# The second product of the last pair of token blocks as seven block products

## The chip, the cores and the metric

The kernel runs on one core of one Trainium2 chip. The metric is the device time of one execution in microseconds (us); three runs of the kernel before gave 1180.23, 1180.44 and 1181.78 us, median 1180.44. The engines are called as the profile calls them: PE is TensorE's matmul side and PEld its weight loads, DVE is VectorE, ACT is ScalarE, POOL is GpSimd, and SP issues the transfers.

## What is computed

Attention with a short window and block summaries runs first; its output is a matrix `x` of 3072 tokens by 512. A mixture of four experts follows, and it holds nearly all the matmul work:

```python
def _moe_ref(x, domain_probs, w1, w2):
    p = domain_probs / (domain_probs.sum(-1, keepdims=True) + 1e-09)
    for e in range(E):                      # E = 4
        h = np.maximum(x @ w1[e], 0.0)      # 512 -> 1024, the first product
        out += p[:, e:e+1] * (h @ w2[e])    # 1024 -> 512, the second product
```

## The kernel before, in words

The tokens are cut into 8 blocks of 384 (`TB`). Blocks 0 and 1 are done with plain products in 32-bit operands. The other six make three pairs (`PAIRS`, line 893), each pair going through the four experts in the order that is listed there; pair 3 takes experts 3, 2, 1, 0. In the pairs every operand is scaled and split in two 16-bit floats, a high part and the rest, and a product of two matrices is three matmul passes: high by high, high by rest, rest by high.

**First product of a pair** (`first`, line 1025). For one expert it goes over four blocks of 256 hidden columns (`order`, four values of `i`). Each block is a 2x2 block product done in seven block products instead of eight (Strassen's scheme in Winograd's form, `SEVEN`, line 989): seven groups of six matmuls with 384 columns. The sums of blocks that it needs are made ahead: those of `x` in `x_operands` (line 453) and those of `w1` in `w1_operands` (line 816). Four PSUM banks a, b, c, d hold the running sums. After product 0, ACT copies bank a to b; after product 1 it copies d to a tile in SBUF; DVE makes c from b after product 2 and d from b after product 4. So product 2 waits for the copy that follows product 0, and product 4 for DVE's reading of b after product 2. Each finished quarter goes through `to_h` (line 855): ACT writes the high part with the Relu, DVE the rest.

**Second product** (`mm2`, line 867). For each of the six tiles of 128 tokens in a pair, 8 hidden groups by 3 passes make 24 matmuls of 512 columns into one bank; DVE then adds the bank, times the mixing weight, to the tile's sum `acc` (line 888), and after the last expert SP stores it (line 890). In `pair_units` (line 994) the second product of one expert is interleaved with the first product of the next; that of the last expert stands alone. The high and low parts of `w2` were made for pair 1, stored to DRAM, and are read back for pairs 2 and 3 (`w2_scaled`, line 776; `fetch2`, line 919), one transfer for two hidden groups. The expert that ends one pair begins the next, and its `w2` stays in place.

**What sets the order.** The program is written as generators that yield after each piece of matmul work, and attention's steps are placed between by their due times; all of attention is done by the end of pair 2. What is written is then ordered by a scheduler at build time: it gives every engine a list in which an instruction may stand well before its written place, as soon as its inputs and a free buffer are there; pieces inside `tc.high_priority` (line 1059) go first. On the chip each engine runs its list in order, so an instruction that waits holds up all that stands behind it. Buffers are counted by tag: 8 of tag `w2`, 14 of tag `x` (`NX`), 7 of tag `w1`, 4 raw weight tiles `wr`, and 16 each of `hh` and `hl`.

Of the kernel before, what the change touches and what calls it, by code (L numbers as in the profile page):

```python
# [26 lines left out]
TB = 384  # L27
NTB = B * S // TB
KC = DM // P
FC = DF // P  # L30
# [13 lines left out]
NX = 14  # L44
# [18 lines left out]
def attn_moe(ctx: ExitStack, tc: tile.TileContext, qvL, qv0, v0L, kD, kT, vT, w1L, w2L, dpL, cst, out):  # L63
# [18 lines left out]
    V, A, PL, PE = (Engine(e, "rest") for e in (nc.vector, nc.scalar, nc.gpsimd, nc.tensor))  # L82
    SP = Engine(nc.sync, "load")

    def pool(name, bufs=1, **kw):
        return ctx.enter_context(tc.tile_pool(name=name, bufs=bufs, **kw))
# [7 lines left out]
    sb = pool("sb")  # L94
    ps_mm = pool("ps_mm", 4, space=bass.MemoryType.PSUM)
    ps_sc = pool("ps_sc", 2, space=bass.MemoryType.PSUM)
    ps_av = pool("ps_av", 2, space=bass.MemoryType.PSUM)
# [9 lines left out]

    X_TOP, W1_TOP = 8.0, 0.25  # L110
    V_TOP = 256.0
    ones = const.tile([2, P], F32, name="ones")
    V.memset(ones, 1.0)
# [1 line left out]
    scale_w, back_w, scale_v, back_x = {}, {}, {}, {}  # L115
# [307 lines left out]
    def x_half(name, dtype=F32R):  # L423
        return sb.tile([P, 2, TB], dtype, name=name, tag="x", bufs=NX)
# [26 lines left out]
    XS = ("11", "21", "22", "t1", "t2", "t3", "t4")  # L451

    def x_operands(pr):
        xp = {w: [x_half(f"x{v}{pr}_{w}", F16) for v in "hl"] for w in XS}

        def split(w, raw, c, lo):
            hi, low = (x[:, :, c : c + QB] for x in xp[w])
            A.copy(hi, raw)
            lo.tensor_tensor(low, raw, hi, op=ALU.subtract)

        def part(ib):
            raw = sb.tile([P, 4, 2, QB], F32, name=f"xr{pr}_{ib}", tag="chunk", bufs=CHUNKS)
            SP.dma_start(raw, xraw.pop((pr, ib)))
            b11, b12, b21, b22 = (raw[:, k] for k in range(4))
            c = ib * QB
            split("11", b11, c, PL)
            V.tensor_tensor(b11, b12, b11, op=ALU.subtract)
            split("22", b22, c, PL)
            V.tensor_tensor(b12, b22, b12, op=ALU.subtract)
            V.tensor_tensor(b22, b22, b11, op=ALU.subtract)  # L470
            split("t2", b22, c, V)
            split("t1", b11, c, PL)
            split("t3", b12, c, V)
            split("21", b21, c, PL)
# [260 lines left out]
    RUSH = 200  # L735
    SLOW = 0.6
    US1, US2 = 0.175, 0.231

    def load_weights(src, e, fc, which):
        raw = sb.tile([P, 512], F32, name=f"wr{which}{e}_{fc}", tag="wr", bufs=4)  # L740
        SP.dma_start(raw, src[e, fc])
        return raw
# [73 lines left out]
    def w1_operands(e, pr):  # L816
# [30 lines left out]
            later(8, SP.dma_start, stored[e, pr, "1"][j], group)  # L847
        return ws

    acc, added = {}, {}  # L850
    scaled_pw = {}
    xpair = {}
    kept = {}
# [37 lines left out]
        yield done, 1.0  # L891

    PAIRS = ((1, (3, 2, 1, 0)), (2, (0, 1, 2, 3)), (3, (3, 2, 1, 0)))

    es_of = dict(PAIRS)
    orders, todo, ready = {}, [], {}
    before = None
    for pr, es in PAIRS:  # L900
        for e in es:
# [11 lines left out]
                return  # L913


    todo2 = [(pr, e, j) for pr, es in PAIRS for e in es for j in range(FC // 2) if pr == 1 or e != es[0]]
    ready2 = {}

    def fetch2():
        if todo2:  # L920
            pr, e, j = todo2.pop(0)
            ready2.setdefault((pr, e), {}).update(w2_scaled(e, j))
# [9 lines left out]
    def tile_by_tile(tbs, e, hT, w2):  # L932
        for tb in tbs:
            for t in range(TB // P):
                yield from mm2(tb, e, [t], hT, w2, range(FC))
# [9 lines left out]
    def plain_units(tbs, e, early=0, last=False):  # L945
# [43 lines left out]
    SEVEN = (  # L989
        ("a", "11", "11"), ("d", "s1", "t1"), ("b", "s2", "t2"), ("a", "12", "21"),  # L990
        ("b", "s3", "t3"), ("c", "s4", "22"), ("b", "22", "t4"),
    )

    def pair_units(pr, es, last=False):


        tbs = (2 * pr, 2 * pr + 1)
        behind = None
        for n, e in enumerate(es):
            hT = {}  # L1000
            w2 = kept.pop(e)[1] if pr > 1 and e in kept else ready2.setdefault((pr, e), {})
            kept.clear()
            units = first(pr, tbs, e, hT, w2, "hl"[n % 2])
            if behind is None:
                for us in units:
                    yield us, SLOW
            else:
                todo_us = 0.0
                for us in units:
                    yield us, 1.0  # L1010
                    todo_us += us * second_share
                    while todo_us > 0.0:
                        us2, _ = next(behind, (todo_us, 0))
                        todo_us -= us2
                        if _:
                            yield us2, 1.0
                yield from behind
            if n < len(es) - 1:
                behind = tile_by_tile(tbs, e, hT, w2)
        kept[e] = {}, w2  # L1020
        yield from with_fetch(second(tbs, e, hT, w2, last))

    second_share = 2 * (TB // P) * FC * 3 * US2 / (2 * FC * 3 * KC * US1 * 7 / 8)

    def first(pr, tbs, e, hT, w2, room):
        xp = xpair[pr]
        room_h = "h" + room
        scaled_pw[e] = sb.tile([P, S // P, 1], F32, name=f"pw{pr}_{e}", tag="pws", bufs=3)
        V.tensor_scalar(
            scaled_pw[e], pw[:, pr * (S // P) : (pr + 1) * (S // P), e : e + 1], back_w[e], back_x[pr],  # L1030
            op0=ALU.mult, op1=ALU.mult,
        )
        order = orders[pr, e]
        for n, i in enumerate(order):
            fetch((pr, e, i))
            if n < len(order) - 1:
                fetch((pr, e, order[n + 1]))
            elif e != es_of[pr][-1]:
                fetch()
            f1, f2 = 2 * i, 2 * i + 1  # L1040
            bank = {}

            def new(k):
                room, tag = dict(a=(ps_sc, "sc"), d=(ps_av, "av")).get(k, (ps_mm, "mm"))
                bank[k] = room.tile([P, 512], F32, name=f"ph{k}{pr}_{e}_{i}", tag=tag)[:, :TB]
                return bank[k]

            for m, (k, w, x) in enumerate(SEVEN):
                first = m < 2
                o = new(k) if first else bank[k]  # L1050
                wh, wl = (ready[pr, e, i][w][:, v * 256 : (v + 1) * 256].rearrange("p (c f) -> p c f", f=P) for v in range(2))
                xh, xl = xp[x]
                again = dict(skip_group_check=not first)
                for c in range(2):
                    PE.matmul(o, wh[:, c, :], xh[:, c, :], start=c == 0 and first, stop=False, **again)
                    PE.matmul(o, wh[:, c, :], xl[:, c, :], start=False, stop=False, **again)
                    PE.matmul(o, wl[:, c, :], xh[:, c, :], start=False, stop=c == 1, **again)
                ahead_of = ExitStack()
                ahead_of.enter_context(tc.high_priority(offset=RUSH))
                if m == 0:  # L1060
                    A.copy(new("b"), o)
                elif m == 1:
                    five = sb.tile([P, TB], F32, name=f"p5{pr}_{e}_{i}", tag="hs", bufs=2)
                    A.copy(five, o)
                elif m == 2:
                    V.tensor_tensor(new("c"), o, five, op=ALU.add)
                elif m == 3:
                    to_h(hT, tbs[0], e, f1, o, room_h)
                elif m == 4:
                    V.tensor_tensor(bank["d"], o, five, op=ALU.add)  # L1070
                    to_h(hT, tbs[1], e, f2, bank["d"], room_h)
                elif m == 5:
                    to_h(hT, tbs[1], e, f1, o, room_h)
                else:
                    to_h(hT, tbs[0], e, f2, o, room_h)
                ahead_of.close()
                if m == 3:
                    if len(w2) < FC:
                        fetch2()
                yield 6 * US1  # L1080
# [3 lines left out]
    for n in range(per, NTB * per):  # L1084
        k = n + SHIFT * (n >= 2 * per)
# [11 lines left out]
    for b in range(1, B):  # L1097
        k = 2 * per * b + SHIFT
        steps += [(k - 2.0, setup_k, b), (k - (0.65 if b == 1 else 1.3), setup_v, b)]
    steps.sort(key=lambda s: s[0])  # L1100
    at = 0
# [18 lines left out]

    plan = [([0], (0, 1)), ([1], (1, 0)), ([0, 1], (2, 3)), *PAIRS]
    pos = per
    for (tbs, experts), end in zip(plan, ENDS):
        pair = tbs if isinstance(tbs, int) else None
        n = 2 if pair else len(tbs)
# [5 lines left out]
        parts, u, done = None, 0.0, 0.0  # L1131
# [82 lines left out]
```

## Time and profile before

| | |
|---|---|
| median of three runs | 1180.44 us |
| the profiled execution, first to last instruction | 1179.2 us |
| pair 3, first matmul to last matmul | 941.6 to 1175.2 us |
| the lone second product at the end of pair 2 | 910.9 to 941.5 us |
| pairs 1 and 2, roughly | 380 to 620 and 620 to 910 us |

The profiled execution's own span, 1179.2 us, is 1.2 us below the median. The page gives busy time for each engine over the span and in 40 slices of 29.5 us; a digit is the busy share in tenths. A row of a group reads: line, engine, operation, what is written from what, shape, count, then busy time, the mean duration of one, and the idle time before. Nearly all rows say L75, since a helper on that line issues every operation, so the tile names tell them apart: `po` are the banks of the second product, `pha` to `phd` those of the first product in pairs, `h` the split hidden values, `wr` raw weights, `w1g` and `w2s` prepared weights, `p` the tile that holds the copy of d.

### The profile page before, as it was taken

To read this page: it belongs to the slowest core of one execution; us is meant where nothing else is said; L and a number is where in the kernel's file an instruction comes from. 1 tells how busy PE (TensorE), PEld (TensorE's weight loads), DVE (VectorE), ACT (ScalarE), POOL (GpSimd) and SP (SyncE) were. 2 spreads that over 40 slices of the span, in tenths; PEclk is the share of its full clock that TensorE was granted. 3 is DMA by queue.
4 is the path that set the end of the run, shared out by engine and by line. 5 is a ranking of instruction groups with operands and counts; after the bars stand their busy time and mean duration, and the time that the engine had idled before them with its cause. 6 is when DMAs were issued, how large, how long until landed. Compare 5 with 4: busy or idle time off the path is not lost.

```text
span 1179.2 us, 19097 instructions
## 1 busy us (share of the span) xinstructions
PE 1114.9 (95%) x6562; PEld 715.7 (61%) x6562; DVE 709.1 (60%) x1767; ACT 598.4 (51%) x1682; POOL 455.3 (39%) x554
## 2 busy tenths in 40 slices
PE   9899698999999888989979999999999999999998
PEld 7788587798897544444545455555555455555553
DVE  6877879875889767666886754554455343322221
ACT  5767466664557687777664454444443132111110
POOL 2588466762736777675642321222111100000000
PEclk9999889999999899999989999999999999999999
DMA  6576656653845767786773554463633132324001
GB/s 240 157 207 181 172 155 185 171 155 92 250 110 150 227 214 261 245 251 209 229 250 110 176 149 135 126 191 111 201 103 96 64 118 72 118 86 122 28 1 54
DMA packets 166417, 181.90 MB, mean 154 GB/s; under 512 B 79024, under 2 KB 114864, under 8 KB 166320
## 3 DMA queue, kind: packets, MB, share of 16 engines
q1 hardware_dynamic: 166320, 180.69, 51.3%
q8 instruction: 51, 0.84, 0.3%
q14 instruction: 46, 0.38, 0.1%
HBM read 129.66 MB, written 34.08 MB: 139 GB/s over the span
## 4 chain that ended last, share of the span: by engine, by line
PE 46%; DVE 3%; DMA 2%; issue 0%; ACT 0%; POOL 0%; DVEq 0%
PE po L75 24%; PE phb L75 9%; PE pha L75 6%; PE phd L75 3%; PE phc L75 3%; PE psc L75 1%; DMA vch<-in_vT 1%; PE px L75 1%; DMA xr<-xd 1%; DVE xr L75 0%; DVE acc L75 0%; DVE xl_t L75 0%; DVE vsr L75 0%; DVE ksr L75 0%; DVE h L75 0%
## 5 line engine op out<-in xcount | busy, mean ns | idle before, releaser
L75 PE MATMUL po<-w2s,h 128*128 128x512 f16 x1728 | 403.8, 379 | 0.2 <-DVE acc L75 0.2
L75 PEld LDWEIGHTS <-w1g 128*128 128x128 f16 x2016 | 196.2, 99 | 175.9 <-issue 32.4
L75 PEld LDWEIGHTS <-h 128*128 128x128 f16 x1728 | 166.0, 98 | 182.0 <-issue 0.8
L75 PE MATMUL phb<-xh_t,w1g 128*128 128x384 f16 x576 | 165.2, 330 | 13.3 <-DVE phc L75 7.4
L75 PE MATMUL ph<-xh,w 128*128 128x384 f32 x512 | 143.8, 352 | 10.2 <-POOL w L75 4.8
L75 POOL TENSOR_TENSOR ks<-kr,ks 128x304 fp32r<-128x304 f32 x112 | 99.2, 891 | 102.8 <-ACT ks L75 102.2
L75 PE MATMUL po<-w,hh 128*128 128x512 f32 x384 | 121.6, 395 | 0.0
L75 PE MATMUL pha<-xh,w1g 128*128 128x384 f16 x384 | 110.9, 332 | 8.5 <-DVE nb L75 7.5
L75 ACT ACTIVATE ms<-ms,nb 96x152 f32<-96x152 f32 x256 | 104.2, 414 | 24.4 <-DVE nb L75 23.8
L75 PEld LDWEIGHTS ph<-xh,w 128*128 128x128 f32 x512 | 97.7, 197 | 12.6 <-POOL w L75 5.2
L75 POOL TENSOR_TENSOR w<-wr,w 128x512 fp32r<-128x512 f32 x60 | 81.6, 1368 | 54.5 <-ACT w L75 52.9
L75 PE MATMUL phb<-xl_t,w1g 128*128 128x384 f16 x288 | 94.9, 330 | 0.0
L75 POOL TENSOR_TENSOR v<-qv,v 128x256 f16<-128x256 f32 (+1 forms) x56 | 43.1, 771 | 132.5 <-ACT v L75 115.2
L75 DVE SCALAR_TENSOR_TENSOR acc<-po,pw,acc 128x512 f32<-128x512 f32 x72 | 52.8, 744 | 68.8 <-PE po L75 68.4
L75 DVE CUSTOM_DVE_ANT_0 ms<-psc,c_sb 96x152 f32<-96x152 f32 x256 | 69.4, 305 | 33.0 <-PE psc L75 32.0
L75 PE MATMUL ph<-xl,w 128*128 128x384 f32 x256 | 88.7, 346 | 0.0
L75 PEld LDWEIGHTS po<-w,hh 128*128 128x128 f32 x384 | 70.6, 188 | 14.4
L75 PE MATMUL po<-w,hl 128*128 128x512 f32 x192 | 76.3, 398 | 0.0
L75 DVE TENSOR_TENSOR aw<-ms,aw 96x512 f16<-96x512 f32 x112 | 69.6, 655 | 9.3 <-ACT aw L75 9.0
L75 ACT CAST aw<-ms 96x512 f16<-96x512 f32 x112 | 49.4, 488 | 48.5 <-issue 27.0
L75 PE MATMUL psc<-ks,qs 128*96 128x152 f32 x448 | 64.5, 270 | 4.5 <-POOL qs L75 4.5
L75 ACT CAST ks<-kr 128x304 fp32r<-128x304 f32 x112 | 48.1, 442 | 39.7 <-PE psc L75 37.8
(155 smaller groups left out, 1894.5 us busy)
## 6 DMA issues: line engine op xcount, KB each, us to landing
wr<-in_w1L SPq DMA_DIRECT2D x76, 256.0 KB, 3.2
wr<-in_w2L SPq DMA_DIRECT2D x72, 256.0 KB, 3.7
qv<-in_qvL SPq DMA_DIRECT2D x56, 320.0 KB, 3.6
kr<-in_kD SPq DMA_DIRECT2D x56, 256.0 KB, 3.3
w1g<-wdg SPq DMA_DIRECT2D x28, 512.0 KB, 3.5
w2s<-wd SPq DMA_DIRECT2D x24, 512.0 KB, 4.4
w1g<-wdg SPq DMA_DIRECT2D x28, 384.0 KB, 3.3
wdg<-w1g SPq DMA_DIRECT2D x16, 512.0 KB, 3.9
```

The lines of the kernel that those rows point to most:

```text
L75: ins = getattr(self.engine, name)(*a, **kw)
```

## The change

In pair 3 alone (`SEVENS = (3,)`) the second product is done in seven block products too. The two token blocks are the two rows of blocks, each two groups of 128 hidden units the two inner blocks, and the two halves of the 512 output columns the two columns of blocks. For each expert and each of three tiles of 128 tokens per token block, seven groups of 12 matmuls with 256 columns replace 2 x 24 matmuls with 512. The sums of `h` are made in `h_operands` right behind the products of the first product, in place of `to_h`. The sums of `w2` are made on chip from raw weights in `w2_operands`, once for each of 16 (expert, block): `fetch7` is called four times in the first product of expert 3, and four times in each second product for the expert that follows. In pair 3, first and second product are written one after the other and no longer interleaved. Three smaller edits belong to it: the operands of `x` are held as 7 tiles of double width instead of 14 (a tile of tag `x` has room for both parts), the scale `X_TOP` is 4 instead of 8, and pair 3's `w2` is no longer read back from DRAM (12 transfers).

```diff
+    SEVENS = (3,)
-        xp = {w: [x_half(f"x{v}{pr}_{w}", F16) for v in "hl"] for w in XS}
+        both = {w: sb.tile([P, 2, 2, TB], F16, name=f"x{pr}_{w}", tag="x", bufs=NX) for w in XS}
+        xp = {w: (x[:, 0], x[:, 1]) for w, x in both.items()}
...
+    def w2_operands(e, i):
+        groups = [
+            sb.tile([P, 4, 512], F16, name=f"w2g0{e}_{i}", tag="w2", bufs=FC),
+            sb.tile([P, 3, 512], F16, name=f"w2g1{e}_{i}", tag="x", bufs=NX),
+        ]
+        ws = {w: groups[j][:, n, :] for j, names in enumerate(TS) for n, w in enumerate(names)}
+        r1, r2 = (load_weights(w2L, e, 2 * i + j, "2") for j in range(2))
+        for raw in (r1, r2):
+            A.mul(raw, raw, scale_w[e][1])
...
+        def parts(w, raw, lo):
+            hi, low = ws[w][:, 0:256], ws[w][:, 256:512]
+            A.copy(hi, raw)
+            lo.tensor_tensor(low, raw, hi, op=ALU.subtract)
+
+        parts("11", b11, PL)
+        V.tensor_tensor(b11, b12, b11, op=ALU.subtract)
+        parts("22", b22, PL)
+        V.tensor_tensor(b12, b12, b22, op=ALU.subtract)
+        V.tensor_tensor(b22, b22, b11, op=ALU.subtract)
+        parts("t1", b11, V)
+        parts("21", b21, PL)
+        parts("t2", b22, V)
+        PL.tensor_tensor(b21, b21, b22, op=ALU.subtract)
+        parts("t3", b12, V)
+        parts("t4", b21, PL)
...
+    def second_sevens(pr, tbs, e, hs):
+        for t in range(TB // P):
...
+            for m, (k, h, w) in enumerate(SEVEN):
+                first = m < 2
+                o = new(k) if first else bank[k]
+                for i in range(FC // 2):
+                    hh, hl = (x[:, t * P : (t + 1) * P] for x in hs[i, h])
+                    wh, wl = w2_sums[e, i][w]
+                    PE.matmul(o, hh, wh, start=i == 0 and first, stop=False, **again)
+                    PE.matmul(o, hh, wl, start=False, stop=False, **again)
+                    PE.matmul(o, hl, wh, start=False, stop=i == FC // 2 - 1, **again)
+                with tc.high_priority(offset=RUSH):
+                    if m == 0:
+                        A.copy(new("b"), o)
+                    elif m == 1:
+                        five = sb.tile([P, 256], F32, name=f"q5{pr}_{e}_{t}", tag="hs", bufs=2)
+                        A.copy(five, o)
+                    elif m == 2:
+                        V.tensor_tensor(new("c"), o, five, op=ALU.add)
+                    elif m == 3:
+                        add(0, 0, "a")
+                    elif m == 4:
+                        V.tensor_tensor(bank["d"], o, five, op=ALU.add)
+                        add(1, 1, "d")
+                    elif m == 5:
+                        add(0, 1, "c")
+                    else:
+                        add(1, 0, "b")
+                    if e == es_of[pr][-1] and m > 4:
+                        gt = gts[m - 5]
+                        SP.dma_start(out[gt * P : (gt + 1) * P, :], acc.pop(gt))
+                if m in (1, 5) and t < 2:
+                    fetch7()
...
+    def h_operands(pr, e, i, m, src, at):
...
+        if m in (3, 4):
+            w = "11" if m == 3 else "22"
+            at[w] = temp("r" + w, "kr" if m == 3 else "qv")
+            A.activation(at[w], src, AF.Relu)
+            parts(w, at[w], PL)
+        elif m == 5:
+            s1, s3, s2 = temp("s1", "ms"), temp("s3", "kl"), temp("s2", "awT")
+            V.scalar_tensor_tensor(s1, src, 0.0, at["22"], op0=ALU.max, op1=ALU.add)
+            V.scalar_tensor_tensor(s3, src, 0.0, at["11"], op0=ALU.max, op1=ALU.subtract)
+            parts("s1", s1, V)
+            V.tensor_tensor(s2, s1, at["11"], op=ALU.subtract)
+            parts("s3", s3, PL)
+            parts("s2", s2, PL)
+            at["s2"] = s2
+        else:
+            hi, low = op("12")
+            A.activation(hi, src, AF.Relu)
+            V.scalar_tensor_tensor(low, src, 0.0, hi, op0=ALU.max, op1=ALU.subtract)
+            s4 = temp("s4", "kr")
+            V.scalar_tensor_tensor(s4, src, 0.0, at["s2"], op0=ALU.max, op1=ALU.subtract)
+            parts("s4", s4, V)
```

`parts` in `h_operands` is the same pair of operations as in `w2_operands`, on 384 columns: ACT copies to the high part, the named engine makes the rest. `second_sevens` makes each bank tile as wide as a PSUM bank and uses its first 256 columns.

More of the change, by code (lines that the diff above doesn't have):

```diff
@@ L105, in attn_moe @@
     gsel = [c_sb[:NST, C_G + j : C_G + j + 1] for j in range(3)]
-    X_TOP, W1_TOP = 8.0, 0.25
+    X_TOP, W1_TOP = 4.0, 0.25
     V_TOP = 256.0
@@ L848, in w1_operands @@
         return ws
+    TS = ("11", "t1", "t2", "21"), ("t3", "22", "t4")
+    w2_sums = {}
+    def w2_operands(e, i):
[7 more added lines that the diff above has]
+            A.mul(raw, raw, scale_w[e][1])
+        b11, b12 = r1[:, 0:256], r1[:, 256:512]
+        b21, b22 = r2[:, 0:256], r2[:, 256:512]
+        def parts(w, raw, lo):
[13 more added lines that the diff above has]
+        parts("t4", b21, PL)
+        w2_sums[e, i] = {w: (x[:, 0:256], x[:, 256:512]) for w, x in ws.items()}
     acc, added = {}, {}
@@ L913, in fetch, with fetch7 @@
                 return
-    todo2 = [(pr, e, j) for pr, es in PAIRS for e in es for j in range(FC // 2) if pr == 1 or e != es[0]]
+    todo2 = [
+        (pr, e, j) for pr, es in PAIRS for e in es for j in range(FC // 2)
+        if (pr == 1 or e != es[0]) and pr not in SEVENS
+    ]
+    todo7 = [(e, i) for pr, es in PAIRS if pr in SEVENS for e in es for i in range(FC // 2)]
+    def fetch7():
+        if todo7:
+            w2_operands(*todo7.pop(0))
     ready2 = {}
@@ L997, in pair_units @@
         tbs = (2 * pr, 2 * pr + 1)
+        if pr in SEVENS:
+            for e in es:
+                hs = {}
+                kept.clear()
+                for us in first(pr, tbs, e, hs, None, None):
+                    yield us, 1.0
+                yield from second_sevens(pr, tbs, e, hs)
+            return
         behind = None
@@ L1023, in attn_moe, with new, add @@
     second_share = 2 * (TB // P) * FC * 3 * US2 / (2 * FC * 3 * KC * US1 * 7 / 8)
+    def second_sevens(pr, tbs, e, hs):
+        for t in range(TB // P):
+            bank = {}
+            def new(k):
+                room, tag = dict(a=(ps_sc, "sc"), d=(ps_av, "av")).get(k, (ps_mm, "mm"))
+                bank[k] = room.tile([P, 512], F32, name=f"po{k}{pr}_{e}_{t}", tag=tag)[:, :256]
+                return bank[k]
+            gts = [tb * (TB // P) + t for tb in tbs]
+            if e == es_of[pr][0]:
+                for gt in gts:
+                    acc[gt] = sb.tile([P, DM], F32, name=f"acc{gt}", tag="acc", bufs=6)
+            def add(row, col, k):
+                gt = gts[row]
+                pe = scaled_pw[e][:, gt % (S // P)]
+                to = acc[gt][:, col * 256 : (col + 1) * 256]
+                if e == es_of[pr][0]:
+                    V.tensor_scalar_mul(to, bank[k], pe)
+                else:
+                    V.scalar_tensor_tensor(to, bank[k], pe, to, op0=ALU.mult, op1=ALU.add)
+            for m, (k, h, w) in enumerate(SEVEN):
+                first = m < 2
+                o = new(k) if first else bank[k]
+                again = dict(skip_group_check=not first)
+                for i in range(FC // 2):
[26 more added lines that the diff above has]
+                    fetch7()
+                yield 12 * US2 / 2, 1.0
+        for i in range(FC // 2):
+            w2_sums.pop((e, i))
@@ new lines, in h_operands, with temp, op, parts @@
+    def h_operands(pr, e, i, m, src, at):
+        def temp(name, tag):
+            return sb.tile([P, TB], F32, name=f"{name}{pr}_{e}_{i}", tag=tag, bufs=2)
+        def op(w):
+            tag = "hl" if w in ("s2", "s3", "s4") else "hh"
+            t = sb.tile([P, 2, TB], F16, name=f"h{w}{pr}_{e}_{i}", tag=tag, bufs=2 * FC)
+            at["ops"][i, w] = t[:, 0, :], t[:, 1, :]
+            return at["ops"][i, w]
+        def parts(w, raw, lo):
+            hi, low = op(w)
+            A.copy(hi, raw)
+            lo.tensor_tensor(low, raw, hi, op=ALU.subtract)
+        if m in (3, 4):
[12 more added lines that the diff above has]
+            at["s2"] = s2
+        else:
+            hi, low = op("12")
[4 more added lines that the diff above has]
+            parts("s4", s4, V)
@@ L1025, in first @@
     def first(pr, tbs, e, hT, w2, room):
         xp = xpair[pr]
-        room_h = "h" + room
+        sevens = pr in SEVENS
+        room_h = None if sevens else "h" + room
         scaled_pw[e] = sb.tile([P, S // P, 1], F32, name=f"pw{pr}_{e}", tag="pws", bufs=3)
@@ L1041, in first @@
             bank = {}
+            at = dict(ops=hT)
             def new(k):
@@ L1066, in first @@
                     V.tensor_tensor(new("c"), o, five, op=ALU.add)
+                elif sevens:
+                    if m == 4:
+                        V.tensor_tensor(bank["d"], o, five, op=ALU.add)
+                    h_operands(pr, e, i, m, bank["d"] if m == 4 else o, at)
                 elif m == 3:
@@ L1076, in first @@
                 ahead_of.close()
-                if m == 3:
+                if sevens:
+                    if e == es_of[pr][0] and (n, m) in ((0, 0), (0, 3), (1, 2), (2, 1)):
+                        fetch7()
+                elif m == 3:
                     if len(w2) < FC:
```

## The prediction

> **What bounds the kernel now.** I read the page first, its parts 1 and 2.
>
> ```profile
> span 1179.2 us, 19097 instructions
> ...
> PE 1114.9 (95%) x6562; PEld 715.7 (61%) x6562; DVE 709.1 (60%) x1767; ACT 598.4 (51%) x1682; POOL 455.3 (39%) x554
> ...
> PE   9899698999999888989979999999999999999998
> ...
> DVE  6877879875889767666886754554455343322221
> ACT  5767466664557687777664454444443132111110
> POOL 2588466762736777675642321222111100000000
> PEclk9999889999999899999989999999999999999999
> ```
>
> The share of 95% says little by itself; the slices say where it is full. From slice 22 on PE is at 9 in each, at full clock, while DVE, ACT and POOL fall to 2, 1 and 0. The last pair, which the change touches, lies there. Next I asked for the busy time by stage: pair 1, pair 2, the lone second product that ends pair 2, and pair 3. Columns: length, then busy time of PE, PEld, DVE, ACT and POOL with their counts, clock, DMA share, GB/s.
>
> ```profile
> 380.00:620.00 240.00, 208.88 (x1214) 116.48 (x1214) 171.10 (x389) 176.84 (x478) 162.48 (x194) 0.96 0.75 234
> 620.00:910.00 290.00, 289.79 (x1765) 156.44 (x1763) 154.24 (x402) 132.07 (x394) 66.12 (x94) 1.00 0.47 137
> 910.90:941.50 30.60, 30.60 (x144) 13.87 (x142) 10.41 (x23) 5.32 (x17) 4.71 (x8) 1.00 0.21 74
> 941.60:1175.20 233.60, 233.60 (x1249) 122.00 (x1247) 70.75 (x123) 44.83 (x96) 0.00 (x0) 1.00 0.24 76
> ```
>
> In pair 3 PE is busy for 233.60 of 233.60 us. So the end is set by how much PE has to stream there, and DVE has 163 us to spare, ACT 189, POOL all of it. The chain of waits gives the pace; its rows are start, length, what, count.
>
> ```profile
> 956.41 1.95 PE phb L75 x12
> ...
> 1146.38 28.94 PE po L75 x134
> ```
>
> A matmul of 384 columns takes 1.95 / 12 = 162.5 ns, one of 512 columns 28.94 / 134 = 216.0 ns. Pair 3 has 4 experts x 4 blocks x 42 = 672 of the first and 4 x 6 x 24 = 576 of the second: 109.2 + 124.4 = 233.6 us, which is the row above to the tenth. Nothing else is on the path. Behind the last matmul stand one sum on DVE and one store:
>
> ```profile
> 1175.34 0.75 DVE L75 SCALAR_TENSOR_TENSOR acc<-po,pw,acc 128x512 f32<-128x512 f32 x1 [4.43 <-PE po L75]
> 1176.12 0.33 SPq L75 DMA_DIRECT2D out_dram<-acc  x1
> ```
>
> I work against this execution's 1179.2 us; the median of the runs is 1.2 us more, and the difference found here is put on the median, 1180.4.
>
> **Part 1: the matmuls.** The 576 of 512 columns go, and 4 experts x 3 tiles x 7 x 12 = 1008 of 256 columns come. The profile has no 128x128 16-bit matmul of 256 columns. From the two paces, 128 columns cost 53.5 ns, so 256 columns should take 162.5 - 53.5 = 109.0 ns. 1008 x 109.0 = 109.9 us in place of 124.4: **-14.5 us**. Seven eighths of the columns would be -15.6; the shorter matmuls give 1 us of that back.
>
> This holds if the weight load, one for each matmul, still fits under the matmul before it.
>
> ```profile
> L75 PEld LDWEIGHTS <-w1g 128*128 128x128 f16 x2016 | 196.2, 99 | 175.9 <-issue 32.4 <-POOL w1g L75 2.2 <-ACT w1g L75 2.1
> L75 PEld LDWEIGHTS po<-w,hh 128*128 128x128 f32 x384 | 70.6, 188 | 14.4
> L75 PEld LDWEIGHTS pmw<-c_sb,wm 128*2 128x2 f32 x4 | 0.3, 80 | 0.7 <-DVE xs L75 0.7
> ```
> ```profile
> 378.32 0.40 PE L75 MATMUL po<-w,hl 128*128 128x512 f32 x1
> 378.56 0.62 PE L75 MATMUL po<-w,hh 128*128 128x512 f32 x2
> 379.01 0.40 PE L75 MATMUL po<-w,hl 128*128 128x512 f32 x1
> ```
>
> A 16-bit load of 128 columns is recorded with 99 ns, and loading just 2 columns with 80, so most of the 99 is latency and some 20 ns are the load itself. The bad case is in the 32-bit rows: 188 ns of load under a 512-column matmul, and three matmuls take 379.01 - 378.32 = 0.69 us, 230 ns each, 14 ns over the 16-bit pace. 99 of 109 ns is as tight a fit as 188 of 216, so the bounds are 0 and 14 ns, 0 to 14.1 us for 1008. I take 0, since the 16-bit load leaves no trace at 384 columns. [...]
>
> **Part 2: sums of h.** Per block of the first product (42 x 162.5 ns = 6.83 us of PE) `to_h` went four times; now seven operands are made. The rows of one operation each:
>
> ```profile
> L75 ACT CAST w1g<-wr 128x256 f16<-128x256 f32 x112 | 42.0, 399 | 10.9 <-POOL wr L75 10.7
> L75 ACT CAST qs<-qv 128x384 fp32r<-128x384 f32 x56 | 28.5, 509 | 5.4 <-DMA qv<-in_qvL 3.1 <-PE psc L75 2.1
> L75 ACT ACTIVATE h<-phc 128x384 f16<-128x384 f32 x48 | 23.2, 484 | 12.2 <-PE phc L75 12.0
> L75 ACT ACTIVATE wr<-wr,scalew 128x512 f32<-128x512 f32 x16 | 11.5, 720 | 9.3 <-DMA wr<-in_w2L 8.7 <-DVE w1g L75 0.5
> ```
> ```profile
> L75 DVE SCALAR_TENSOR_TENSOR acc<-po,pw,acc 128x512 f32<-128x512 f32 x72 | 52.8, 744 | 68.8 <-PE po L75 68.4
> L75 DVE TENSOR_TENSOR w1g<-wr,w1g 128x256 f16<-128x256 f32 x64 | 36.5, 574 | 28.2 <-ACT w1g L75 27.8
> L75 DVE TENSOR_TENSOR phc<-phb,p 128x384 f32<-128x384 f32 x48 | 26.9, 561 | 39.4 <-PE phb L75 25.0 <-issue 9.1 <-ACT p L75 4.6
> L75 DVE SCALAR_TENSOR_TENSOR h<-pha,h 128x384 f16<-128x384 f32 x48 | 26.5, 552 | 36.4 <-ACT h L75 36.3
> L75 DVE TENSOR_TENSOR w<-wr,w 128x512 fp32r<-128x512 f32 x24 | 18.4, 774 | 1.3 <-ACT w L75 1.3
> ```
> ```profile
> L75 POOL TENSOR_TENSOR w1g<-wr,w1g 128x256 f16<-128x256 f32 x48 | 37.3, 788 | 29.0 <-ACT w1g L75 28.9
> L75 POOL TENSOR_TENSOR wr<-wr 128x256 f32<-128x256 f32 x32 | 27.5, 859 | 14.7 <-DVE w1g L75 14.0
> L75 POOL TENSOR_TENSOR w2s<-wr,w2s 128x512 f16<-128x512 f32 x16 | 21.1, 1316 | 13.5 <-ACT w2s L75 13.5
> ```
>
> ACT: two copies and three Relus from PSUM at 0.484, six casts at 0.509: 5.5 us. DVE: two bank sums at 0.561, four operations from PSUM at 0.552, three of 384 columns from SBUF, between 0.574 (256) and 0.774 (512), say 0.67: 5.3 us. POOL: four of 384 columns between 0.788 and 1.316, say 1.05: 4.2 us. Each stays under 6.83, so none becomes the bound by itself. The tight places are the waits inside a block: PE returns to bank b after one group of 0.975 us, in which ACT's copy takes 0.484 or DVE's sum 0.561. About 0.4 us of cover is left, and an operation of some other kind that has just begun can use it up.
>
> At the passage to the second product, s1 of the last block is ready 0.552 + 0.509 + 0.67 = 1.73 us after its product, against 0.975 + 12 x 0.109 = 2.28 us of matmuls that don't need it. s2 comes later (0.552 + 0.552 + 0.67 + 0.67 on DVE, 0.509, 1.05: 4.0 us against 3.59), 0.4 us short, 1.6 us for four experts at most; the next tile's first group can run in between, so I take 0 and keep 1.6.
>
> **Part 3: sums of w2.** One preparation is, on ACT, 2 x 0.720 + 7 x 0.399 = 4.2 us; on DVE 6 x 0.574 = 3.4; on POOL 4 x 0.788 + 0.859 = 4.0. There are 16. With 16 blocks of part 2 and 12 token tiles of the new second product (ACT 2 x 0.48; DVE six of 256 columns, between half of 0.744 and 0.561, say 0.45), pair 3 needs: ACT 87 + 68 + 12 = 167 us, DVE 85 + 55 + 32 = 172, POOL 67 + 64 = 131, beside 109.2 + 109.9 = 219.1 us of PE. The four preparations for expert 3 need not wait for pair 3, because the lists run ahead of the written order:
>
> ```profile
> 906.20 3.88 SPq L75 DMA_DIRECT2D w2s<-wd  x3
> ...
> 942.80 0.46 ACT L75 COPY phb<-pha 128x384 f32<-128x384 f32 x1 [19.33 <-PE pha L75]
> ```
>
> These w2 loads are for pair 3's second expert and are written inside its first product, which begins at 941.6 + 27.3, some 60 us later; they went out as soon as buffers came free. The new preparations get buffers at the same time. The lone second product of 30.6 us leaves ACT 25, DVE 20 and POOL 26 us free, against 17, 14 and 16. So I cost them at nothing. If that cover fails, ACT has 4 x (5.5 + 4.2) = 39 us in the first 27.3 us, and PE waits 4 us (t4 is needed last, 8 us into the second product) to 11.5.
>
> The other twelve stand beside a full PE, and this is the one cost that I can't call hidden. Pair 1 prepares weights in the same way, 32 preparations (16 of w1, 16 of w2), and its waits show what they do:
>
> ```profile
> ACT wr L75 <- DMA wr<-in_w1L: 17.3, 17, 2.4
> ...
> PE pha L75 <- DVE nb L75: 7.5, 2, 7.2
> PE phb L75 <- DVE phc L75: 7.4, 5, 2.4
> ...
> PE phb L75 <- ACT phb L75: 4.2, 4, 1.8
> ...
> PE phb L75 <- DVE phd L75: 1.8, 2, 1.5
> ```
>
> ACT's list stands still until raw weights land; DVE waits for ACT's cast; the bank sum that PE needs is queued behind. PE lost 7.4 + 4.2 + 1.8 = 13.4 us in this way, 0.42 for each preparation. Pair 2, with no preparations but with attention, lost 290.00 - 289.79 = 0.2 us. So twelve cost between 0 and 12 x 0.42 = 5.0 us if the rates carry over. Pair 3 has lighter DMA traffic than pair 1 (76 against 234 GB/s), but its first product runs without second-product matmuls between, so evacuations come twice as densely. I take the upper value, **+5.0 us**, and leave room above it.
>
> **Part 4: the rest.** The last sum on DVE is 256 columns wide, about 0.45 in place of 0.75: **-0.3 us**. Raw weights (32 transfers of 256 KB, 8 MB) replace 12 of 512 KB (6 MB) on an SP queue that carries 76 GB/s here: nothing. Seven double tiles in place of fourteen free half of tag `x` earlier, so pair 3's x sums move forward into pair 2, where PE lost 0.2 us in all: nothing, give or take 1 us for a changed order in pair 1. The scale edit costs nothing.
>
> Sum: -14.5 + 5.0 - 0.3 = -9.8; 1180.4 - 9.8 = **1170.6 us**.
>
> **The rivals.** *No waits at all*: the scheduler keeps two blocks in flight and hides everything. For it speaks pair 2. 1180.4 - 14.8 = 1165.6 us. *Heavier waits*, 9 to 14.8 us: the cover under the lone second product fails, or every block loses half a microsecond; 1174.6 to 1180.4. *Weight loads bind* at 256 columns: 0 to 14 ns on 1008 matmuls; with the waits above up to 1170.6 + 14.1 = 1184.7. For it: the 32-bit rows; against it: the 20 ns that a 16-bit load itself takes. *Slower than before*: the preparations hold ACT and DVE in their lists as in pair 1, with no second product beside the first to fill PE. Pair 1 left PE idle for 240 - 208.88 = 31.1 us in 240, 13%; the same share of 219 us is 28 us, 1180.4 - 14.8 + 28 = 1194. It decides when the waits pass 14.8 us, 0.92 us for each of the 16 blocks. For it: ACT at 167 of 219 us is as full as in pair 1 (177 of 240). Against it: 7.5 us of pair 1's idle time come from attention's maxima (`nb`).
>
> **How the numbers follow.** Forecast 0.55 (waits of 1 to 9 us), no waits 0.12, heavier waits 0.13, weight loads 0.08, slower 0.12. A measurement here can tell about 0.2%, 2.4 us. Faster by more: 0.55 + 0.12 + 0.09 of the heavier waits + 0.02 = 0.78. Within it: 0.04 of the heavier waits, 0.02 of the weight loads, 0.03 of the last: 0.09. Slower by more: 0.04 + 0.09 = 0.13. The range goes from 1165.0, no waits with a little won in pair 1, to 1180.5, the end of the heavier waits; it leaves out most of the two last cases.
>
> **What would show it.** Right: in the chain of waits the runs of `po` in pair 3 come out at 109 ns a matmul; PE's busy time from pair 3's first matmul to its last is near 219 us; the idle time before PE is some 5 us, released by `phc`, `phb` or `phd`, behind ACT rows that wait for `wr`; ACT's idle gap of 19.33 us before pair 3 is filled with w2 casts. Wrong: `po` at 115 ns or more (weight loads), PE idle over 10 us in pair 3, or gaps that clock PE down.

## The result and the profile after

The kernel after the change takes 1186.13 us, the median of 10 runs (1182.49 to 1194.57), the kernel before 1180.34 us beside it (1176.64 to 1184.17). The ratio is 1.005, 95% interval 1.0027 to 1.0074: slower by 0.5%, where 0.8% faster was forecast. The profiled execution after takes 1185.91 us.

First the page of the kernel after, its span, busy times and slices:

```profile
span 1184.0 us, 20638 instructions
...
PE 1105.7 (93%) x6994; PEld 757.4 (64%) x6994; DVE 812.9 (69%) x1959; ACT 693.6 (59%) x1930; POOL 581.0 (49%) x698
...
PE   9899698999999879889979999999999999999898
...
DVE  5888779875888667676888354445457674958574
ACT  5767466664557788777676344444445662828251
POOL 2587455772736777686554111223214651827251
```

PE has 9.2 us less to do than before (1114.9), and still the span is longer. In the last third DVE, ACT and POOL no longer fade to 2, 1 and 0. They run in bursts: DVE goes 7, 4, 9, 5, 8, 5, and PE falls from 9 to 8 in one slice there. The stages show it, with the columns of the table in the prediction: pair 2, the lone second product, all of pair 3, and then four pieces of pair 3, the first product of expert 3 and the second product behind it, and the first products of experts 2 and 0, each with the passage that follows.

```profile
620.00:910.00 290.00, 288.63 (x1757) 155.90 (x1756) 159.84 (x416) 138.28 (x417) 75.40 (x107) 1.00 0.47 136
910.50:941.20 30.70, 30.70 (x144) 13.90 (x143) 21.87 (x42) 19.38 (x48) 17.77 (x26) 1.00 0.34 106
941.20:1180.40 239.20, 223.72 (x1681) 164.29 (x1679) 157.67 (x280) 118.16 (x288) 104.14 (x115) 0.99 0.23 76
```
```profile
941.20:976.10 34.90, 30.89 (x182) 18.28 (x181) 25.66 (x45) 23.94 (x55) 19.61 (x22) 0.95 0.43 141
976.10:1006.30 30.20, 30.20 (x267) 25.83 (x265) 13.40 (x26) 7.04 (x19) 4.18 (x6) 1.00 0.07 21
...
1006.30:1034.90 28.60, 25.74 (x163) 15.54 (x160) 27.06 (x47) 25.00 (x65) 24.69 (x29) 1.00 0.54 182
...
1129.50:1156.30 26.80, 26.80 (x179) 17.19 (x176) 21.16 (x36) 18.09 (x41) 15.48 (x18) 1.00 0.03 13
```

Ahead of pair 3 nothing was lost in this execution: it begins at 941.2 us, before at 941.6. Pair 3 takes 239.2 us in place of 233.6. In expert 2's first product DVE is busy for 27.06 of 28.60 us and PE idle for 2.9; in the second product of expert 3 just ahead of it, DVE is busy for 13.40 of 30.20 and PE never idle. So the work that was added lies on top of the sums of h, in the denser of the two stages. In expert 0's first product, the last row, only 4 of the 112 casts of w2 are left to do, and PE is full.

The chain of waits has the pace of the new matmuls, and the list of PE's waits in pair 3 has the rest (microseconds in total, times, longest):

```profile
1152.77 0.97 PE phc L75 x6
...
1160.72 1.31 PE pob L75 x12
```
```profile
PE phb L75 <- ACT phb L75: 7.4, 6, 2.0
PE pod L75 <- DVE hs L75: 4.0, 2, 2.1
PE phb L75 <- DVE phc L75: 2.2, 3, 0.9
PE phb L75 <- DVE phd L75: 1.2, 1, 1.2
PE poa L75 <- ACT h L75: 0.5, 1, 0.5
PE pod L75 <- ACT hs L75: 0.2, 1, 0.2
```

A matmul of 256 columns takes 1.31 / 12 = 109.2 ns, so the stream of pair 3 is 672 x 162.5 + 1008 x 109.2 = 219.3 us, and 239.2 - 219.3 = 19.9 us are lost. The waits are 15.5 of that. The clock took more: behind two of the waits in expert 3's first product it was granted at 0.54 for 3.5 us, in which 12 matmuls went where 21 would have fitted, a loss of some 1.6 us (the other 2.8 us are not placed):

```profile
944.00:947.00 3.00, 1.40 (x9) 0.74 (x8) 3.00 (x8) 2.09 (x6) 1.79 (x3) 1.00 0.59 180
947.00:951.00 4.00, 1.97 (x12) 1.07 (x11) 3.00 (x7) 3.00 (x7) 1.26 (x2) 1.00 0.79 276
951.00:954.50 3.50, 3.49 (x12) 1.71 (x12) 0.57 (x1) 1.61 (x3) 0.91 (x1) 0.54 0.24 92
```

How one wait comes about can be read in the timeline (start, length, engine, what; in brackets the idle time before and its releaser):

```profile
1020.35 1.14 PE L75 MATMUL pha<-x,w1g 128*128 128x384 f16 x6
...
1020.93 1.13 DVE L75 TENSOR_TENSOR wr<-wr,wr 128x256 f32<-128x256 f32 x1
...
1021.75 2.47 POOL L75 TENSOR_TENSOR w2g<-wr,w2g 128x256 f16<-128x256 f32 x3
...
1021.99 1.70 DVE L75 TENSOR_TENSOR w2g<-wr,w2g 128x256 f16<-128x256 f32 x2
...
1023.61 1.01 DVE L75 SCALAR_TENSOR_TENSOR s<-phc,r 128x384 f32<-128x384 f32 x2
...
1024.19 0.51 ACT L75 CAST hs<-s 128x384 f16<-128x384 f32 x1 [1.43 <-DVE s L75]
...
1025.39 0.48 ACT L75 COPY phb<-pha 128x384 f32<-128x384 f32 x1
...
1025.93 0.81 PE L75 MATMUL phb<-x_t,w1g 128*128 128x384 f16 x4 [1.52 <-ACT phb L75]
```

Read it upwards. PE waits 1.52 us for ACT's copy of bank a to b. Its input, bank a, was done about 1021.5 us, yet the copy stands in ACT's list behind casts of h sums. The first of these waited 1.43 us for DVE's `s`. (The copy also writes a bank that must be free: the b and c of all blocks share four banks, and the `s` at 1023.61 reads the c of an earlier block. So the list and the bank lead to the same place.) And `s` stood in DVE's list behind three operations of a w2 preparation, 1.13 and 2 x 0.85 us each, while POOL worked on the same preparation. No DMA is in this chain. The longest wait, 2.04 us in expert 3's first product, is of a mixed kind:

```profile
949.49 0.72 ACT L75 ACTIVATE wr<-wr,scalew 128x512 f32<-128x512 f32 x1 [0.87 <-DMA wr<-in_w2L]
...
950.48 0.48 ACT L75 COPY phb<-pha 128x384 f32<-128x384 f32 x1
951.01 1.81 PE L75 MATMUL phb<-x_t,w1g 128*128 128x384 f16 x6 [2.04 <-ACT phb L75]
```

Here ACT's list stood still for 0.87 us until raw weights had landed, and the copy came behind. In all of pair 3 ACT waited for such transfers three times, 2.1 us in total. It waited longer for DVE's part of the sums and of the preparations:

```profile
ACT hs L75 <- DVE s L75: 10.5, 16, 1.4
ACT w2g L75 <- DVE wr L75: 10.2, 10, 1.8
```

### The profile page after: what moved, and what is told of

Read it like the earlier page. It is cut to its first block, busy times and chain, and to the rows that moved or that the text cites. A ratio compares the mean times of both kernels' runs of the same rounds, so it can differ in the third digit from the quotient of the medians.

```text
span 1184.0 us, 20638 instructions
## 1 busy us (share of the span) xinstructions
PE 1105.7 (93%) x6994; PEld 757.4 (64%) x6994; DVE 812.9 (69%) x1959; ACT 693.6 (59%) x1930; POOL 581.0 (49%) x698
## 4 chain that ended last, share of the span: by engine, by line
PE 48%; DVE 19%; DMA 14%; ACT 9%; POOL 5%; issue 4%; SPq 1%; ACTq 0%; POOLq 0%; DVEq 0%
PE po L75 14%; PE ph L75 6%; PE phb L75 6%; PE pha L75 4%; PE pob L75 4%; DMA wr<-in_w1L 4%; DMA wr<-in_w2L 3%; PE psc L75 3%; PE poa L75 2%; PE phd L75 2%; PE phc L75 2%; ACT wr L75 2%; DMA xr<-xd 2%; DVE wr L75 2%; DVE ms L75 2%
## 5 line engine op out<-in xcount | busy, mean ns | idle before, releaser
L75 PE MATMUL po<-w2s,h 128*128 128x512 f16 x1152 | 271.4, 381 | 1.1 <-DVE h L75 1.1
L75 PEld LDWEIGHTS <-h 128*128 128x128 f16 x1584 | 152.1, 98 | 128.1 <-issue 2.6
L75 PE MATMUL phb<-x_t,w1g 128*128 128x384 f16 x864 | 166.4, 328 | 24.5 <-ACT phb L75 10.8
L75 PE MATMUL pha<-x,w1g 128*128 128x384 f16 x576 | 115.1, 333 | 6.4 <-DVE nb L75 4.8
L75 POOL TENSOR_TENSOR w2g<-wr,w2g 128x256 f16<-128x256 f32 x64 | 47.6, 759 | 101.9 <-ACT w2g L75 101.8
L75 PEld LDWEIGHTS po<-w,hh 128*128 128x128 f32 x384 | 70.9, 189 | 14.5
L75 ACT CAST w<-wr 128x512 fp32r<-128x512 f32 x84 | 50.9, 616 | 32.1 <-DMA wr<-in_w1L 22.1
L75 POOL TENSOR_TENSOR qs<-qv,qs 64x384 fp32r<-64x384 f32 x56 | 58.7, 1049 | 15.6 <-ACT qs L75 11.8
```

Source lines behind the costliest of these rows:

```text
L75: ins = getattr(self.engine, name)(*a, **kw)
```

## The experiments

Theory A: the w2 preparations, run ahead by the lists into the first products, hold up what PE needs there and cost nearly all of the 20 us. Rivals: B, the sums of h cost it alone; C, something of the change moves work ahead of pair 3. Lost time is measured in each profile as the length of pair 3 less 219.3 us, so that it does not depend on where pair 3 begins. That start is spread: 941.6 and 941.8 us in two profiles of the kernel before, 941.2 and 944.6 us in two of the kernel after, 939.6 to 949.8 us in those of the kernels made from it, though ahead of the preparations their instructions stand in the same order as after the change.

**Most preparations left out.** Only expert 3's four are made; experts 2, 1 and 0 multiply with them again.

```diff
-            w2_operands(*todo7.pop(0))
+            e, i = todo7.pop(0)
+            if e == 3:
+                w2_operands(e, i)
...
-                    wh, wl = w2_sums[e, i][w]
+                    wh, wl = w2_sums[3, i][w]
...
```

> The changed kernel, but w2 is prepared for expert 3 alone (in the lone second product of pair 2, as before); the other three experts reuse those operands, so 12 of 16 preparations are left out. Theory A (the w2 preparations, pulled by the scheduler into the first products of pair 3, hold up ACT and DVE and cost nearly all of the 20 us that PE loses there): PE waits in pair 3 fall under 2 us and the time is about 1186.1 - 18 = 1168 us, 1166 to 1170. Theory B (the sums of h by themselves make the dense first product wait): waits of 10 us or more stay, 1176 us or more. Theory C (something moved earlier in the kernel, since all of its order changed): no change, 1184 or more.

Measured: 1171.14 us, ratio 0.9887 (0.9842 to 0.9931). Its pair 3, and the only wait in it:

```profile
939.70:1159.70 220.00, 219.60 (x1681) 164.09 (x1679) 119.17 (x219) 88.77 (x200) 64.98 (x64) 1.00 0.19 61
```
```profile
PE phb L75 <- DVE phc L75: 0.4, 1, 0.4
```

220.0 us, 0.7 lost. All sums of h are still made, so B falls as a sole cause, and expert 3's own four preparations cost nothing.

**The sums of h left out.** The second product reads four plain parts of h again in place of the sums; all 16 preparations stay.

```diff
-                    hh, hl = (x[:, t * P : (t + 1) * P] for x in hs[i, h])
+                    q = dict(s1="21", s2="21", s3="21", s4="12").get(h, h)
+                    hh, hl = (x[:, t * P : (t + 1) * P] for x in hs[i, q])
...
-                    h_operands(pr, e, i, m, bank["d"] if m == 4 else o, at)
+                    src, q = bank["d"] if m == 4 else o, {3: "11", 4: "22", 5: "21", 6: "12"}[m]
+                    both = sb.tile([P, 2, TB], F16, name=f"h{q}{pr}_{e}_{i}", tag="hh", bufs=2 * FC)
+                    hT[i, q] = both[:, 0, :], both[:, 1, :]
+                    A.activation(both[:, 0, :], src, AF.Relu)
+                    V.scalar_tensor_tensor(both[:, 1, :], src, 0.0, both[:, 0, :], op0=ALU.max, op1=ALU.subtract)
```

> The changed kernel with all 16 preparations, but the sums of h are left out: each of the four quarters of h is only split in two parts as in the kernel before, and the seven products use these four. POOL has nothing to do for h then, ACT six and DVE six operations for a block in place of eleven and nine. Theory A: the preparations still stand in the first products' lists, so a good part of the waits stays, 5 to 12 us, 1173 to 1180. Theory B: the waits go, under 2 us, about 1168. If both are needed for the loss (a full list), something near 1170.

Measured: 1177.58 us, ratio 0.9968 (0.9945 to 0.9991); pair 3:

```profile
939.60:1165.90 226.30, 220.15 (x1681) 164.06 (x1679) 114.13 (x232) 83.63 (x207) 37.53 (x51) 1.00 0.25 80
```

226.3 us, 7.0 lost. Preparations alone cost 7, sums of h alone 0.7, both together 20: the two meet in the same lists at the same time. A is right about the place, and needs the addition that the sums of h had used up the room.

**The preparations held.** Nothing is left out. ACT's instructions of each preparation for experts 2, 1 and 0 may not stand ahead of the last cast of h sums, so they fall beside the second product, where they were written.

```diff
-                    fetch7()
+                    with tc.issue_after(last_cast[0]):
+                        fetch7()
...
-            A.copy(hi, raw)
+            last_cast[0] = A.copy(hi, raw).ins
```

> The changed kernel, nothing left out, but ACT's instructions of the preparations for experts 2, 1 and 0 are ordered behind the last h cast of the expert before, so they run beside its second product, not beside its first. Theory A: PE waits in pair 3 fall under 3 us, time 1167 to 1170, faster than the kernel before by 10 to 13 us. Theory B: no better than the changed kernel, 1182 to 1188. Against both: if the second product's own evacuations are as tight, waits move there and the time stays over 1176.

Measured: 1177.88 us, ratio 0.9961 (0.9942 to 0.998). Pair 3 takes 226.4 us, 7.1 lost, and but for one wait of 0.4 us (`phb`) PE no longer waits in a first product:

```profile
PE pob L75 <- DVE poc L75: 3.3, 6, 0.8
PE poa L75 <- DVE acc L75: 0.9, 2, 0.5
PE phb L75 <- DVE phc L75: 0.4, 1, 0.4
...
```

So the same work, moved into the second products, loses about a third as much. What is left is the same fault in another list: DVE's copy into bank c stands behind operations of a preparation.

**The x tiles alone.** The kernel before, with the double x tiles and the new scale and nothing else of the change.

> The kernel before with only the seven double tiles for x and the scale 4, second product plain. Theory A: within 0.3% of the kernel before, 1177 to 1184, pair 3 still starting at 941 +- 3 us and without waits. Theory C: 1184 or more, the loss arising ahead of pair 3.

Measured: 1183.82 us, ratio 0.9999 (0.998 to 1.0019); pair 3 takes 233.7 us without a wait. C falls as far as the x tiles and the scale go; for the kernel after, the profile itself has the loss inside pair 3.

**POOL idle.** All that POOL does in the preparations and in the sums of h is left out: the low parts that it writes, in whose place the matmuls read the high part again, and one difference of w2.

```diff
...
-            lo.tensor_tensor(low, raw, hi, op=ALU.subtract)
+            if lo is V:
+                V.tensor_tensor(low, raw, hi, op=ALU.subtract)
+            else:
+                ws[w] = hi, hi
...
-        PL.tensor_tensor(b21, b21, b22, op=ALU.subtract)
...
```

> Leaves out all that GpSimd does in the last pair's preparations and h sums (its low parts, where the matmul reads the high part a second time, and one difference of w2); TensorE's, ScalarE's and VectorE's instructions stay as they are after the change. Theory contention (VectorE's instructions take about 0.9 us instead of 0.4 to 0.55 because GpSimd works on the same memory at the same time, and it is this lengthening that turns the preparations into waits): the 384-column sums of h fall from a mean of 0.93 us to 0.5 to 0.6 us, and the waits of TensorE in the last pair from 20 us to 4 to 9 us, so that the pair takes 223 to 229 us instead of 239. Rival position (what counts is that ScalarE's and VectorE's lists hold a whole preparation ahead of a copy that TensorE needs, whatever an instruction takes): VectorE gets no quicker or it does not help, 12 us or more of waits stay, the pair takes 231 us or more.

Measured: 1176.17 us, ratio 0.9959 (0.9944 to 0.9974). Pair 3 takes 224.9 us, 5.6 lost. DVE's groups in pair 3 (count, then busy time and mean ns of one), after and with POOL idle:

```profile
L75 DVE TENSOR_TENSOR hs<-s,hs 128x384 f16<-128x384 f32 x32 | 28.4, 898 | 4.0 <-ACT hs L75 3.8
L75 DVE TENSOR_TENSOR w2g<-wr,w2g 128x256 f16<-128x256 f32 x33 | 21.3, 650 | 0.9 <-ACT w2g L75 0.9
L75 DVE SCALAR_TENSOR_TENSOR s<-phc,r 128x384 f32<-128x384 f32 x32 | 16.4, 547 | 3.4 <-ACT r L75 3.4
L75 DVE TENSOR_TENSOR s<-s,r 128x384 f32<-128x384 f32 x16 | 14.0, 878 | 0.0
```
```profile
L75 DVE TENSOR_TENSOR hs<-s,hs 128x384 f16<-128x384 f32 x32 | 17.7, 554 | 8.1 <-ACT hs L75 7.9
L75 DVE SCALAR_TENSOR_TENSOR s<-phc,r 128x384 f32<-128x384 f32 x32 | 16.4, 552 | 4.0 <-ACT r L75 3.1 <-PE pha L75 0.6
L75 DVE TENSOR_TENSOR w2g<-wr,w2g 128x256 f16<-128x256 f32 x33 | 13.2, 419 | 4.8 <-ACT w2g L75 4.8
...
L75 DVE TENSOR_TENSOR s<-s,r 128x384 f32<-128x384 f32 x16 | 8.8, 549 | 0.0
```

Operations whose two inputs both lie in SBUF fall from 898 to 554 ns, 878 to 549 and 650 to 419; the one that reads a PSUM bank stays at 547 and 552. The preparations still stand in the first products, and PE loses 5.6 us instead of 19.9. So without POOL's work beside DVE they are far cheaper. One reservation: with POOL's instructions gone the scheduler also orders the lists a little differently, and nothing waits for POOL any more, so the whole of the 14 us is not shown to be DVE's lengthening.

**Half of the preparations.** Of the twelve for experts 2, 1 and 0, six are made and read twice.

> Half of the preparations of experts 2, 1 and 0 are left out (two of four each, 6 of 12; the second product reads those two twice), everything else as after the change. If every preparation that stands in a first product costs its own wait (20 us less the 0.5 us without them, about 1.6 us each), half of the waits stay: 8 to 12 us, the last pair takes 228 to 231 us, the whole 1175 to 1177 us. If it is a threshold (the lists of a first product have room for some preparations, and it is the last ones that push the sums of h over), less than 5 us stay, the pair takes less than 225 us.

Measured: 1175.43 us, ratio 0.9957 (0.994 to 0.9974); pair 3 takes 225.7 us, 6.4 lost, between the two expectations. Most of it is in expert 3's first product, where no fewer casts of w2 stand than after the change. In expert 2's, with 15 casts of w2 in place of 24, 1.3 us are lost in place of 6.8. The first six cost 5.7 us and the other six 13.5, so they have no fixed price each; a sharp threshold is not shown either.

**The preparations spaced.** As held, and DVE's part is held too, behind its copies into banks c or d; one preparation for each of three token tiles and a fourth in the first (7), or all four in the first two tiles (8).

```diff
...
-                if m in (1, 5) and t < 2:
-                    fetch7()
+                if (t, m) in ((0, 2), (0, 4), (1, 4), (2, 4)):
+                    with tc.issue_after(last_cast[0]), tc.issue_after(dve[0]):
+                        fetch7()
...
```

> Nothing left out: as the kernel with the preparations held (7.2 us of waits, all in second products behind VectorE's copy into bank c), and now one preparation behind the copy into bank d of each of the three token tiles and the fourth behind the first tile's bank c, so that VectorE's list has five block products of 1.31 us until the next copy that TensorE needs. If position in the list is what costs: waits fall to 1 to 5 us, the last pair takes 220 to 225 us, the time is 0.990 to 0.996 of the kernel before. Rival: the engines are simply full in a second product (VectorE 25 of 32 us), then 6 to 8 us of waits stay and the ratio is 0.996 as held. Second rival: the last preparation runs on into the next first product and brings back waits there.

> As the spaced kernel, but the four preparations in the first two token tiles (behind banks c and d of each), so that nothing runs on into the next first product. Position in the list: bank d of the second tile comes behind a preparation, 1 to 2 more waits of 0.5 us for each expert than the spaced kernel, 3 to 7 us in all; if what hurts is the run-on into the next first product, this one is the faster of the two by 1 to 3 us.

Measured: 1177.47 us, ratio 0.9969 (0.9951 to 0.9986), for the first and 1177.77 us, ratio 0.9979 (0.9964 to 0.9993), for the second. Pair 3 takes 225.0 and 227.2 us: 5.7 and 7.9 lost, at the same place as held. Holding DVE is not enough. In both, as in the held kernel, three of DVE's copies into bank c had themselves waited for ACT's copy of the fifth product (`q`):

```profile
DVE poc L75 <- ACT q L75: 3.3, 3, 2.5
```

That is ACT's list again, and the next kernel holds it too.

**Both lists held.** Each preparation is held behind that copy on ACT and behind the copy into bank c or d on DVE, and laid later.

```diff
...
-                        A.copy(five, o)
+                        act[0] = A.copy(five, o).ins
...
-                if m in (1, 5) and t < 2:
-                    fetch7()
+                if (t, m) in ((0, 3), (1, 1), (1, 4), (2, 4)):
+                    with tc.issue_after(act[0]), tc.issue_after(dve[0]):
+                        fetch7()
```

> Nothing left out. The spaced kernel still waits 5.5 us in the last pair's second products, where VectorE's copy into bank c stands behind ScalarE's copy of the fifth product, and that behind casts of w2. Here each preparation is also held behind ScalarE's copy of the fifth product of its token tile, and the four are laid later (first tile after its fourth block product, second after its second and fifth, third after its fifth). If ScalarE's list is what is left: waits of 1 to 4 us, the last pair takes 220 to 224 us, ratio to the kernel before 0.990 to 0.996. Rival: a preparation is as long as the room between two copies (some 4.5 us beside 5 block products of 1.31 us), and what one copy gains the next loses: 5 to 7 us of waits stay, ratio 0.996 to 0.998.

Measured: 1167.76 us (1165.42 to 1175.84), ratio 0.9905 (0.9881 to 0.9929): faster than before by 0.95%, nothing left out. Pair 3, expert 2's two products one after the other, and PE's waits:

```profile
949.80:1170.60 220.80, 219.91 (x1681) 164.24 (x1679) 153.91 (x291) 130.75 (x308) 107.89 (x124) 1.00 0.26 85
```
```profile
1009.20:1036.10 26.90, 26.90 (x179) 17.27 (x178) 21.19 (x37) 18.18 (x43) 15.57 (x18) 1.00 0.41 135
1036.10:1064.50 28.40, 28.14 (x246) 23.87 (x245) 19.82 (x43) 18.04 (x46) 14.98 (x20) 1.00 0.24 77
```
```profile
PE pob L75 <- DVE poc L75: 0.5, 2, 0.3
PE phb L75 <- DVE phc L75: 0.4, 1, 0.4
```

DVE, ACT and POOL do no less of the work in pair 3 than after the change (DVE is busy for 153.91 us against 157.67, ACT for 130.75 against 118.16), and 1.5 us are lost in place of 20. The work is even now: DVE 21.19 of 26.90 us in the first product and 19.82 of 28.40 in the second, where it was 27.06 of 28.60 and 13.40 of 30.20. POOL works beside DVE here too (107.89 us), so its work alone does not make PE wait. Against the spaced kernels two things changed at once, the hold on ACT's list and the places of the four; what each gave was not told apart.

**Both kernels once more.**

> The changed kernel once more, beside the spaced one on the same chip. If its waits are a property of its lists and not of one execution, the last pair again takes 237 to 241 us with about 20 us of waits at the same copies. The last pair began at 941.2 us in its first profile, and at 939.6 to 947.9 us in the profiles of the kernels made from it, whose instructions stand in the same order up to there; if that is spread between executions, its start lies anywhere in this span. Rival: the kernels made from it lose some 4 us ahead of the last pair, then it begins at 940 to 942 us again.

> The kernel before once more. Its last pair takes 233 to 234 us, with less than 1 us of waits. Its start shows what of the start's spread is the chip's: between 939 and 948 us if executions differ, 941 to 942 us if they do not.

Measured: after 1189.3 us, ratio 1.0068 (1.0044 to 1.0092), pair 3 from 944.6 us, 241.5 us long, with the same list of waits (6.9, 4.0, 2.2, 1.2 us at the same copies); before 1180.44 us, ratio 1.001 (0.9996 to 1.0025), pair 3 from 941.8 us, 233.7 us long, no wait. The waits belong to the lists, not to one execution.

What stays open: the held and the spaced kernels shorten pair 3 by 7.3 and 8.7 us and the time by 4 to 5 and 3 to 4; the kernel with both lists held shortens pair 3 by 12.9 and the time by 11 to 12. The difference lies ahead of pair 3. There the kernels made from the change have the order of the kernel after, but from about 355 us on not that of the kernel before, and executions of one kernel are as far apart as that (1165.42 to 1175.84 us). Part of it goes with the clock: of the six executions of the kernel with both lists held, the longest, which is the profiled one, has a mean granted clock of 0.973, the two shortest 0.979. Whether the rest is more than spread was not settled.

## Why the prediction was wrong

**Part 1 was right.** Forecast were 109.0 ns and -14.5 us; the matmul takes 109.2 ns, and the stream of pair 3 is 219.3 us in place of 233.6, -14.3. The weight load, 98 ns by its record beside the matmuls of 256 columns, adds nothing that shows, and the rival in which it binds is out.

**Part 2 was right as it was put, and misleading.** The sums of h cost 0.7 us when little else is there (the bounds given for the passages to the second product: 0 to 1.6). In the kernel after, with the preparations beside them, the passages alone cost 4.0 + 0.5 + 0.2 = 4.7 us of waits (`pod` and `poa`). And its sum for DVE, 5.3 us in 6.83 for each block, took 0.67 us for a 384-column operation from SBUF, which came to 0.90 beside POOL; and what it showed, that DVE is 78% full in a first product, was then not used in part 3.

**Part 3 is the step that failed.** The four preparations for expert 3 cost nothing, as said. For the other twelve pair 1's rate was carried over, 0.42 us each, 5.0 in all; they cost 239.2 - 220.0 = 19.2 us, 1.6 each. Three things were wrong in it. The load was held against the whole pair (DVE 172 of 219 us), though the same paragraph had found that the lists run ahead of the written order: the preparations, written into second products, ran into first products, whose DVE had no room. The part named the danger ("evacuations come twice as densely") and put no number on it. The row for DVE's preparations came from pair 1, where the like shape took 574 ns; here it took 650. And the mechanism was given as ACT's list standing still until raw weights land. That had the smaller part: ACT waited 2.1 us for transfers in all of pair 3, 0.87 of them ahead of PE's longest wait, but 10.5 us for DVE's `s` and 10.2 for DVE's `wr`, and the 1.52 us wait followed above goes back to DVE's list.

**The rival that came true** is the one called slower than before: preparations holding ACT's and DVE's lists with no second product beside the first to fill PE. Its point of decision, 14.8 us of waits, was passed (19.9). It was given a chance of 0.12, on the ground that pair 1's idle time was in part attention's. Its price, 28 us, was too high. Its argument, ACT at 167 us, was too high as well: ACT is busy for 118.16 us in pair 3, with six of the 16 preparations made ahead of it; the fuller list was DVE's.

**Part 4 was right.** The tail behind the last matmul is 3.6 us (3.9 before), and the x tiles alone change nothing (0.9999).

## What to carry to other kernels

When work is added beside a full PE, sum each engine's load by stage, and in the stage where the lists will put it, not where it is written; here a stage in which DVE was 95% full stalled PE though its mean over the pair was 66%. What can be prepared early needs an upper bound on how early: here one ordering constraint on each of two lists, with the preparations laid later, turned a loss of 0.5% into a gain of 0.95%. And a constraint on one list moves the wait to the next one, so look again at who is late after each.

## What the runs showed of the hardware

Over pair 3, in which POOL is busy for 104 of 239 us, the DVE operations with both inputs in SBUF took on average some 1.6 times as long as with POOL idle (898 against 554 ns at 384 columns, 650 against 419 at 256); those that read a PSUM bank did not (547 against 552, and 558 against 564 for the same TENSOR_TENSOR when it makes bank c from b). Single ones took longer: the 19 of the 32 `hs<-s,hs` that had POOL working for nine tenths of their time or more took 1.05 us on average. In busy time the three groups shown come to 28.4 + 21.3 + 14.0 us against 17.7 + 13.2 + 8.8, 24 us of pair 3. The prediction had not looked for it. By what means POOL's work lengthens them, no run here shows.

The second is a lower clock behind waits, which in the kernel after cost time on top of that in which PE stood still: behind two waits for ACT's copy to bank b (1.60 and 2.04 us), with PE busy for 3.37 of 7 us, the next 3.5 us were granted 0.54 of full speed, some 1.6 us more lost. In its second profile, with the same list of waits, the mean granted clock over pair 3 is 0.98, against 0.99 in the first and 1.00 in the kernel before. But such waits did not always bring it: in the kernel with half of the preparations PE waited 3.9 us for the same copy, in two waits of which the longer took 2.1 us, and the mean over pair 3 is 1.00. What decides it is not shown. In the kernel with both lists held, where the waits come to 0.9 us, it is 1.00 in pair 3 too.
